# An attention and FFN block on one core: K in two rings of 512-key tiles, thinner FFN filling, one matmul for the rows of -max

## The chip, the core and the metric

One NeuronCore of a Trainium2 chip runs the whole kernel in one launch. TensorE (PE) multiplies matrices into eight PSUM banks, VectorE (DVE) and ScalarE (ACT) work on SBUF and PSUM, GpSimd (POOL) on SBUF alone; SyncE (SP) and POOL issue most DMAs. The engines run side by side, each in the order of its own instructions, and wait for each other by semaphores. The metric is the device time of one execution in microseconds, from the first to the last instruction.

## What is computed

A block with adaptive layer norm: attention with 32 heads of 16 channels over 2048 tokens of 512 channels, and a gated FFN with 1792 hidden channels, all in float32. The reference, cut:

```python
qkv = (x @ wqkv).reshape(B, S, 3, H, Dh)          # S = 2048, H = 32, Dh = 16
p = softmax(einsum("bhqd,bhkd->bhqk", q, k) * Dh ** -0.5)
A = einsum("bhqk,bhkd->bhqd", p, v)               # ... @ wo
B = (silu(h @ w_gate) * (h @ w_up)) @ w_down
mod = silu(c) @ w_mod                             # sa, ca, ga, sb, cb, gb
x = x + ga * A(layernorm(x) * (1 + ca) + sa)
x = x + gb * B(layernorm(x) * (1 + cb) + sb)
```

Operands of most matmuls are split in a high and a low part; three products (high-high, high-low, low-high) give each result.

## The kernel before, in words

**Stages.** First the projections to q, k, v: q and k go to DRAM in split parts, v stays in SBUF. Then attention in 32 units of 16 steps. A unit is 512 query rows (a chunk, four of them) and one group of four heads; units 0 to 7 are chunk 0, and so on. A step is one key tile of 128 keys for the four heads, in four pairs. After the last unit a tail finishes chunk 2 and does chunk 3's output projection and FFN.

**A pair** (pair_of) is two matmuls side by side on PE, on different 64 rows of the array: a score matmul (L506) of the current unit, with 48 split channels and 2 more rows that hold -max, and a max matmul (L479) some 20 steps ahead. ACT takes the exp of the score (L508), DVE the maximum over 512 keys of the other (L481). When a unit's maxima are complete, max_rows turns them to rows by matmuls with `ident` and `minus` (L491 to L493), and a DMA on SP puts them into the two rows of `qop`, four to five steps before that unit's first score.

**PV** (pv_step, L521) multiplies probabilities by v, in column tiles of 32; half a step at a time ("half"), two steps behind the scores.

**Plain and filled.** Where no FFN work is ready, plain runs windows of three pairs and one or two halves of PV; scores have three PSUM banks (4, 5, 6), max matmuls four. filled runs a group: pairs, with so many terms of an FFN job behind each as a tuple says, then up to six halves of PV. One term is two matmuls side by side on 64 rows each (L718), called a filler pair here. In a group banks 3 and 6 hold the job's sums, scores have banks 4 and 5 only, max matmuls 0 to 2. `TWO = (0, 3, 2, 2, 2, 2, 1, 0)` is a group of eight pairs (two steps) with 12 filler pairs, `ONE = (0, 3, 3, 0)` one of four pairs with 6. A gate_up job (24 filler pairs) takes two TWO, a down job (12) two ONE. A job accumulates in two half phases: in the first, sum 0 takes rows 0 to 63 and sum 1 rows 64 to 127, in the second the other way round. In TWO and ONE the half phase changes where a group ends, with PV between.

**Order around it.** The emitted order is the program's own (manual schedule). STARTS gives the step at which a finished chunk's output projection (out_pair) begins: four TWO groups, then NORM plain steps and three for layer norm, then the FFN jobs, then plain steps to the next chunk. The last 20 steps have no max matmuls; there ALONE exchanges the tuples.

**Unit end** (close_unit). The sums of exps come out of PV; SP fetches them into `dn` (L532), K and q of three units ahead start, DVE takes the reciprocal three steps later (L536), it goes to DRAM and back as `rb`, POOL multiplies (L548) and stores. Seven steps after a chunk's last unit its output is loaded again, two later split.

**Memory.** K of one head group lies in one of three tiles `kop` of 2048 keys; activations (`oT`, `hT`) in one pair `act`.

Of the kernel before, what the change touches and what calls it, by code (L numbers as in the profile page):

```python
# [19 lines left out]
P = 128  # L20
# [26 lines left out]
REST = 24  # L47
NORM = 9
STARTS = (147, 275, 403)
TWO = (0, 3, 2, 2, 2, 2, 1, 0)  # L50
ONE = (0, 3, 3, 0)
ALONE = {TWO: ((0, 4, 0, 4, 0, 4, 0, 0), (4, 5, 0, 1, 5, 0, 4, 1)), ONE: ((0, 6, 0, 0), (4, 5, 4, 0))}

# [48 lines left out]
def block_kernel(ctx, tc, x, wqkv, wo, w_gate, w_up, w_down, c, w_mod, out):  # L102
# [22 lines left out]
    minus = const.tile([P, P], F32, name="minus")  # L125
    eps_t = const.tile([P, 1], F32, name="eps_t")
    quad = const.tile([P, 1], F32, name="quad")
    modc = const.tile([P, 4, NK], F32, name="modc")
# [86 lines left out]
    kop = [vp.tile([P, 2, S], F32R, name="kop0"), None, None]  # L215
# [47 lines left out]
    nc.gpsimd.tensor_scalar_mul(minus, ident, -1.0)  # L263
# [137 lines left out]
    def load_parts(dst, src, g, c0, c1, second=nc.sync):  # L401
        heads = src[g * 64:(g + 1) * 64, :, c0:c1].rearrange("(s b d) r c -> b (d r) s c", s=2, b=2)
        for b in range(2):
            (second if b else nc.sync).dma_start(dst[64 * b:64 * b + KR].bitcast(F32), heads[b])

    def load_k0(ci):
        load_parts(kop[0][:, :, ci * CW:(ci + 1) * CW], kd, 0, ci * CW, (ci + 1) * CW)
# [3 lines left out]
    for b in range(2):  # L411
        nc.sync.dma_start(kop[0][64 * b + KR:64 * b + KR + 2].bitcast(F32).rearrange("p s (a c) -> p (s a) c", c=CW),
                          ones[:, None, :].to_broadcast([2, 2 * NC, CW]))
    kq = [(w, m) for m in range(NK) for w in (1, 0)]
    for ci in range(NC - 1):
# [12 lines left out]
        for i, _ in enumerate(sm.jobs(jobs)):  # L428
# [6 lines left out]
            if i == 40:  # L435
                load_k0(ci)
# [13 lines left out]
    kop[1] = pb.tile([P, 2, S], F32R, name="kop1", bufs=1)  # L450
    pf = None
    qop, mx, pts, pv, o_, due, res = {}, {}, {}, {}, {}, {}, {}
    posts = []
    n = 16 * NU
    last = NC - 1

    def ones_rows(k):
        for b in range(2):
            rows = slice(64 * b + KR, 64 * b + KR + 2)
            nc.sync.dma_start(kop[k][rows].bitcast(F32), kop[0][rows].bitcast(F32))  # L460

    def load_k(u):
        load_parts(kop[u % 3], kd, u % NG, 0, S, nc.gpsimd if u > 2 else nc.sync)

    def load_q(u):
        ci, g = divmod(u, NG)
        qop[u] = pb.tile([P, 2, CW], F32R, name="qop", tag="qop", bufs=3)
        load_parts(qop[u], qd, g, ci * CW, (ci + 1) * CW, nc.gpsimd if u > 2 else nc.sync)

    def max_one(r):  # L470

        u, t = divmod(r // 4, 16)
        b, e = 1 - r % 4 // 2, r % 2
        s, qt, kc = t // 8, t // 2 % 4, t % 2 * 2 + e
# [4 lines left out]
        nc.tensor.matmul(pm, qop[u][rows, s, qt * P:(qt + 1) * P], kop[u % 3][rows, s, kc * CW:(kc + 1) * CW],  # L479
# [3 lines left out]
    def max_rows(u):  # L483
# [3 lines left out]
        nm = pb.tile([P, 16], F32R, name="nm", tag="nm")  # L487

        def rows():
            pr = bank("pr")[0:16, 0:2 * P]  # L490
            nc.tensor.matmul(pr[:, 0:P], nm.bitcast(F32), ident, start=True, stop=True)  # L491
            nc.tensor.matmul(pr[:, P:2 * P], m, minus, start=True, stop=False)
            nc.tensor.matmul(pr[:, P:2 * P], nm.bitcast(F32), minus, start=False, stop=True)  # L493
            mr = pb.tile([16, 2, P], F32R, name="mr", tag="mr", bufs=1)
            nc.scalar.copy(mr, pr.rearrange("p (r q) -> p r q", r=2))
            for r in range(2):
                nc.sync.dma_start(qop[u][KR + r:KR + r + 65:64].bitcast(F32), mr[:, r, :].bitcast(F32))
        side.extend([lambda: None, lambda: None, lambda: nc.scalar.mul(nm, m, -1.0), lambda: None, rows])

    def score(i, h):  # L500
# [5 lines left out]
        nc.tensor.matmul(sp, kop[u % 3][rows, h // 2, kt * P:(kt + 1) * P], qop[u][rows, h // 2, :],  # L506
# [120 lines left out]
    class Chunk:  # L627
# [15 lines left out]
        def load_wo(self, places=None):  # L643
            self.wo = places or [as_wo(tile_gu()) for _ in range(NK // 2)]
            for k, w in enumerate(self.wo):
                (nc.sync if self.ci == 0 else nc.gpsimd).dma_start(w.bitcast(F32), wo_dr[k])

        def load_gu(self, f):
            if f < NF and f not in self.loaded:
                self.loaded.add(f)  # L650
                self.w[f] = self.places[f % len(self.places)] if self.places else tile_gu()
                nc.sync.dma_start(self.w[f].bitcast(F32), gu_dr[f])
# [56 lines left out]
    def accumulate(outs, lhs, rhs, nk, after, halves, by_k=False):  # L709
# [3 lines left out]
        if halves:  # L713
            for ph in range(2):
                for j, (k, a, b) in enumerate(terms):
                    for e in range(2):
                        rows = slice(64 * (ph ^ e), 64 * (ph ^ e) + 64)
                        nc.tensor.matmul(outs[e], lhs(e, a, k)[rows], rhs(b, k)[rows],  # L718
                                         start=(ph == 0 and j == 0), stop=(ph == 1 and j == z))
# [32 lines left out]
    def out_pair(ch, t0, outs, halves):  # L752
        return accumulate(outs, lambda e, a, k: ch.oT[a][:, k, (t0 + e) * P:(t0 + e + 1) * P],
                          lambda b, k: ch.wo[k // 2][:, b, k % 2, :], NK,
                          lambda: posts.append(lambda: add_o(ch, t0, outs, True)), halves)

    def out_terms(ch, t, pt, ks):
        for k in ks:
            for a, b in ((0, 0), (0, 1), (1, 0)):
                nc.tensor.matmul(pt, ch.oT[a][:, k, t * P:(t + 1) * P], ch.wo[k // 2][:, b, k % 2, :],  # L760
                                 start=(k == 0 and a == b == 0), stop=(k == NK - 1 and a == 1))

    def gate_up(ch, f, outs, halves):
# [5 lines left out]
        def after():  # L769
# [3 lines left out]
            def later():  # L773
# [10 lines left out]
        return accumulate(outs, lambda e, a, k: w[:, 2 * e + a, k, :], lambda b, k: ch.hT[b][:, k, :], NK, after,  # L784
                          halves)

    def down(ch, m, t0, outs, halves):
# [7 lines left out]
        def after():  # L795
# [4 lines left out]
            if t0:  # L800
# [4 lines left out]
                          lambda b, k: wd[:, b, k, :], FG, after, halves, m == NF // FG - 1)  # L805
# [4 lines left out]
    def begin(ci):  # L810
        x2 = pf.tile([P, 4, D], F32, name="x2", tag="x2", bufs=1)
# [247 lines left out]
```

## Time and profile before

| what | value |
|---|---|
| three runs, median (lowest to highest) | 1922.31 us (1921.94 to 1923.35) |
| the profiled execution, span | 1926.2 us |
| PE, DVE, ACT, POOL busy | 1876.4, 1541.1, 1250.8, 418.6 us |
| mean granted TensorE clock | 0.984 |
| step 0 to 147 (chunk 0's attention) | 188.3 to 566.3 us |
| last unit's end, tail | about 1762 us, to 1926.2 |

The span is that of one execution; it is 0.2% over the median. Rows of a timeline give start, duration, engine, line, operation, tiles, shapes, count and, in brackets, the idle time before and what ended it. A window's row gives its length, then for each engine the busy time with the number of instructions, then the granted clock, the DMA share and GB/s. "bank" is any PSUM bank. PEld is PE's weight load.

### The profile page before, as it was taken

How to read it: one execution, taken by the hardware profiler on the slowest of the kernel's cores; microseconds unless marked ns; L12 is line 12 of the kernel's file. 1: busy time of each engine (PE TensorE's matmuls, PEld its weight loads, DVE VectorE, ACT ScalarE, POOL GpSimd, SP SyncE). 2: the span in 40 equal slices, each digit the busy share in tenths (PEclk: the TensorE clock that was granted, in tenths of full speed). 3: DMA queues.
4: the chain of work that ended last, by engine and by line, in shares of the span. 5: the costliest groups of instructions: out<-in, count | busy, mean ns of one | idle time of the engine just before them, and what ended most of it. 6: DMA issues, size and time to landing. Idle time of an engine off the chain costs nothing.

```text
span 1926.2 us, 40835 instructions
## 1 busy us (share of the span) xinstructions
PE 1876.4 (97%) x16996; PEld 1149.1 (60%) x16996; DVE 1541.1 (80%) x2558; ACT 1250.8 (65%) x2330; POOL 418.6 (22%) x504
## 2 busy tenths in 40 slices
PE   7999999999999999999899999999899999999999
PEld 5766444444455666666455666666455466667787
DVE  5458998999989888888789888888799988841643
ACT  4222887788877766667677766776677876674211
POOL 3000344555322211111123111111133011021200
PEclk9999999999999999999899999999899999999999
DMA  8764766667753534553544544453543354253642
GB/s 299 265 219 121 187 161 161 190 180 185 192 90 74 141 99 113 148 133 84 130 81 90 121 114 131 116 141 76 135 81 76 54 141 119 73 177 122 237 194 109
DMA packets 78340, 267.60 MB, mean 139 GB/s; under 512 B 17364, under 2 KB 22484, under 8 KB 57476
## 3 DMA queue, kind: packets, MB, share of 16 engines
q1 hardware_dynamic: 58188, 173.81, 31.7%
q0 software_dynamic: 19280, 90.39, 19.5%
q8 instruction: 133, 2.18, 0.5%
q10 hardware_dynamic: 688, 0.80, 0.1%
q14 instruction: 51, 0.42, 0.1%
HBM read 201.85 MB, written 62.13 MB: 137 GB/s over the span
## 4 chain that ended last, share of the span: by engine, by line
PE 89%; DMA 5%; DVE 3%; ACT 2%; SPq 0%; issue 0%; ACTq 0%; DVEq 0%
PE bank L521 25%; PE bank L506 20%; PE bank L718 18%; PE bank L479 9%; PE bank L727 7%; PE bank L209 6%; DMA dn<-o 4%; DVE mx L481 1%; PE bank L760 1%; PE bank L491 1%; DVE stt L743 1%; PE bank L162 0%; PE bank L703 0%; DMA wm_ab<-in_w_mod 0%; PE bank L493 0%
## 5 line engine op out<-in xcount | busy, mean ns | idle before, releaser
L481 DVE TENSOR_REDUCE mx<-bank 128x1 f32<-128x512 f32 x2048 | 1285.6, 683 | 146.9 <-PE bank L479 97.7
L479 PE MATMUL bank<-kop,qop 48*128 48x512 f32 x2048 | 766.2, 439 | 26.4 <-DVE mx L481 25.0
L506 PE MATMUL bank<-qop,kop 50*128 50x512 f32 x2048 | 757.4, 433 | 3.8 <-DMA qop<-mr 0.9
L506 PEld LDWEIGHTS bank<-qop,kop 50*128 50x128 f32 x2048 | 349.0, 187 | 315.6 <-issue 54.5
L479 PEld LDWEIGHTS bank<-kop,qop 48*128 48x128 f32 x2048 | 347.3, 187 | 59.2 <-DVE mx L481 42.4
L718 PE MATMUL bank<-act,wgu 64*128 64x512 f32 x1872 | 295.4, 393 | 0.0
L718 PEld LDWEIGHTS bank<-act,wgu 64*128 64x128 f32 x1872 | 184.3, 187 | 32.6 <-issue 0.2
L548 POOL TENSOR_TENSOR on<-o,rb 128x512 f32<-128x512 f32 x31 | 39.8, 1283 | 527.4 <-DMA rb<-d_dr 379.4
L718 PE MATMUL bank<-wd,mid 64*128 64x512 f32 x912 | 130.5, 392 | 0.0
L779 POOL CAST mid<-m 128x512 fp32r<-128x512 f32 x40 | 24.5, 612 | 345.4 <-PE bank L479 164.8
L209 PE MATMUL bank<-hT,wqs 128*128 128x512 f32 x384 | 95.8, 400 | 2.3 <-ACT hT L328 1.0
L718 PEld LDWEIGHTS bank<-wd,mid 64*128 64x128 f32 x912 | 88.7, 186 | 15.3 <-issue 0.7
L209 PEld LDWEIGHTS bank<-hT,wqs 128*128 128x128 f32 x384 | 70.4, 188 | 24.3 <-issue 6.1
L775 DVE SCALAR_TENSOR_TENSOR q<-th,bank 128x512 f32<-128x512 f32 x56 | 38.1, 681 | 56.8 <-ACT th L771 56.8
L771 ACT ACTIVATE th<-bank 128x512 f32<-128x512 f32 x56 | 33.3, 594 | 58.5 <-PE bank L727 58.4
L791 DVE TENSOR_TENSOR x<-bank,x 128x512 f32<-128x512 f32 x84 | 53.9, 685 | 19.6 <-PE bank L718 19.6
L369 DVE TENSOR_TENSOR prt<-bank,prt 128x512 fp32r<-128x512 f32 x32 | 22.0, 689 | 45.5 <-ACT prt L367 45.5
L367 ACT CAST prt<-bank 128x512 fp32r<-128x512 f32 x32 | 18.8, 586 | 58.6 <-PE bank L209 46.8
L777 DVE TENSOR_TENSOR m<-bank,q 128x512 f32<-128x512 f32 x56 | 38.7, 692 | 21.1 <-PE bank L727 19.1
L727 PE MATMUL bank<-wd,mid 128*128 128x512 f32 x216 | 52.3, 395 | 0.5 <-DVE mid L780 0.3
L780 POOL TENSOR_TENSOR mid<-m,mid 128x512 fp32r<-128x512 f32 x40 | 51.5, 1288 | 3.3
L718 PE MATMUL bank<-wgu,act 64*128 64x512 f32 x288 | 47.9, 395 | 0.1
(6282 smaller groups left out, 5196.9 us busy)
## 6 DMA issues: line engine op xcount, KB each, us to landing
wgu<-gu_dr SPq DMA_DIRECT2D x48, 1024.0 KB
wd<-wd_dr SPq DMA_DIRECT2D x28, 1024.0 KB
kop<-kd SPq DMA_DIRECT2D x33, 768.0 KB
kop<-kd POOLq DMA_DIRECT2D x29, 768.0 KB, 8.4
gu_dr<-wgu POOLq DMA_DIRECT2D x14, 1024.0 KB, 4.9
kd<-prt SPq DMA_DIRECT2D x16, 512.0 KB
qd<-prt SPq DMA_DIRECT2D x16, 512.0 KB
kop<-gu_dr SPq DMA_DIRECT2D x8, 1024.0 KB
```

The costliest lines, as they stand in the source:

```text
L209: nc.tensor.matmul(pt, lhs(a, k), rhs(b, k), start=(n == 0), stop=(n == 3 * nk - 1))
L479: nc.tensor.matmul(pm, qop[u][rows, s, qt * P:(qt + 1) * P], kop[u % 3][rows, s, kc * CW:(kc + 1) * CW], start=True, stop=True)
L481: nc.vector.tensor_reduce(mx[u][:, b, s, qt, kc:kc + 1], pm, op=ALU.max, axis=AX.X)
L506: nc.tensor.matmul(sp, kop[u % 3][rows, h // 2, kt * P:(kt + 1) * P], qop[u][rows, h // 2, :], start=True, stop=True)
L521: nc.tensor.matmul(pv[u][32 * h:32 * h + 32, cols], v_flat[:, e0:e0 + 32], p_[h][:, cols], start=(kt == 0 and half == 0), stop=(kt == 15), ...
L548: mul.tensor_mul(on, o, rb)
L718: nc.tensor.matmul(outs[e], lhs(e, a, k)[rows], rhs(b, k)[rows], start=(ph == 0 and j == 0), stop=(ph == 1 and j == z))
L727: nc.tensor.matmul(outs[e], lhs(e, a, k), rhs(b, k), start=(j == 0), stop=(j == z))
L775: nc.vector.scalar_tensor_tensor(q, th, 1.0, outs[0], op0=ALU.add, op1=ALU.mult)
L777: nc.vector.tensor_mul(m32, outs[1], q)
L780: (nc.gpsimd if slow else nc.vector).tensor_sub(mid[:, 1, :], m32, mid[:, 0, :].bitcast(F32))
L791: nc.vector.tensor_add(ch.x2[:, t, :], outs[e], ch.x2[:, t, :])
```

## The change

Six edits, together:

- **K in two rings.** Three tiles of 2048 keys become two rings of four tiles of 512; each is loaded for the unit two ahead as soon as the unit before has used it (four loads a unit, all on SP, as are q's). Max matmuls now take the key tiles in order.
- **A second pair of activation buffers**, by the parity of the chunk. x and wo of the next chunk are loaded at the end of the chunk's jobs, attention output in pairs of units.
- **Filling over more groups.** Most gate_up jobs take three groups THIN (24 filler pairs in 6 steps), the others two TWO as before; THICK says from which job on. A down job takes one group of eight pairs, DOWN or LATE. The plain steps between chunks and before the last down go; STARTS and REST follow.
- **Half phases inside a group.** Where the half phase changes within a group, ACT copies one column of both sums (`seen`) first, so that the second phase's matmuls come after the first's.
- **One matmul for the rows of -max**, of 32 columns; the low part comes from one DVE operation, and the matmul stands at the end of a window or group (flush).
- **Unit end later**: reciprocal after five steps, not three, and what follows it.

```diff
-STARTS = (147, 275, 403)
+STARTS = (144, 272, 400)
+REST = 12
+THICK = (12, 12, 8)
 TWO = (0, 3, 2, 2, 2, 2, 1, 0)
-ONE = (0, 3, 3, 0)
+DOWN = (0, 3, 3, 0, 0, 3, 3, 0)
+LATE = (0, 0, 3, 3, 0, 0, 3, 3)
+THIN = ((0, 1, 1, 2, 1, 1, 1, 1), (0, 2, 2, 0, 0, 2, 2, 0), (0, 2, 1, 2, 1, 1, 1, 0))
...
-    kop = [vp.tile([P, 2, S], F32R, name="kop0"), None, None]
+    kop = [[vp.tile([P, 2, CW], F32R, name=f"kop0{c}") for c in range(NC)], None]
...
-            pr = bank("pr")[0:16, 0:2 * P]
-            nc.tensor.matmul(pr[:, 0:P], nm.bitcast(F32), ident, start=True, stop=True)
-            nc.tensor.matmul(pr[:, P:2 * P], m, minus, start=True, stop=False)
-            nc.tensor.matmul(pr[:, P:2 * P], nm.bitcast(F32), minus, start=False, stop=True)
+            pr = bank("pr")[0:32, 0:P]
+            nc.tensor.matmul(pr, nm.rearrange("p r h -> p (r h)").bitcast(F32), ident, start=True, stop=True)
...
             for ph in range(2):
+                for e in range(2 if trade and ph else 0):
+                    nc.scalar.copy(seen[:, e:e + 1], outs[e][:, 0:1])
                 for j, (k, a, b) in enumerate(terms):
...
-        at(i + 3, lambda: res.__setitem__(u, out_b(u, nc.sync, *res[u])))
-        at(i + 4, lambda: res.__setitem__(u, out_r(u, nc.sync, *res[u])))
-        at(i + 5, lambda: out_c(u, nc.gpsimd, nc.gpsimd, *res.pop(u)))
...
+        at(i + 5, lambda: res.__setitem__(u, out_b(u, nc.sync, *res[u])))
+        at(i + 6, lambda: res.__setitem__(u, out_r(u, nc.sync, *res[u])))
+        at(i + 8, lambda: out_c(u, nc.gpsimd, nc.gpsimd, *res.pop(u)))
+        if u % 2 and u < NU - 2:
+            at(i + 10, lambda: chunks[u // NG].load_o(nc.gpsimd, (u % NG // 2,)))
+            at(i + 12, lambda: chunks[u // NG].split_o((u % NG // 2,)))
+
+    for u in range(NU - 2):
+        for c in range(NC):
+            at(16 * u + 4 * c + 3, lambda u=u, c=c: load_k(u + 2, c))
...
+    def window(ch, job, args):
+        if job is down:
+            return (LATE if args == (NF // FG - 1, 0) else DOWN,)
+        return (TWO,) * 2 if args[0] >= THICK[ch.ci] else THIN
...
-                plain(WIN)
-            work = job(ch, *args, outs, True)
-            for _ in range(2):
-                filled(TWO if job is gate_up else ONE, work)
+                chunks[ci + 1].load_wo()
+            places = window(ch, job, args)
+            work = job(ch, *args, outs, True, *[True] * (len(places) > 2))
+            for group in places:
+                filled(group, work)
```

What this moves on PE, at a down job of chunk 2. Before, the first half phase ends here and its group with it (bank_66 and bank_69 are the sums, 67 and 68 the scores, 63 to 65 the maxima, 70 PV):

```order
L718 MATMUL bank_69<-wd,mid 128x512
L506 MATMUL bank_68<-qop,kop_1425 128x512 [waits Activation_49]
L479 MATMUL bank_63<-kop_87,qop 128x512 [waits DVE_49]
L521 MATMUL bank_70<-pt__15178,v_flat 32x256
L521 MATMUL bank_70<-pt__15194,v_flat 32x256
L521 MATMUL bank_70<-pt__15183,v_flat 32x256
L521 MATMUL bank_70<-pt__15207,v_flat 32x256
```

And now, at the same place of a job:

```order
L729 MATMUL bank_69<-wd,mid 128x512
L504 MATMUL bank_68<-qop,kop_88 128x512 [waits Activation_49]
L474 MATMUL bank_63<-kop_971,qop 128x512 [waits DVE_49]
L504 MATMUL bank_67<-qop,kop_88 128x512 [waits Activation_49]
L474 MATMUL bank_64<-kop_971,qop 128x512 [waits DVE_49]
L504 MATMUL bank_68<-qop,kop_88 128x512 [waits Activation_49]
L474 MATMUL bank_65<-kop_971,qop 128x512 [waits DVE_49]
L729 MATMUL bank_66<-wd,mid 128x512 [waits Activation_49]
L729 MATMUL bank_69<-wd,mid 128x512 [waits Activation_49]
```

The PV between the half phases is gone; three pairs without filling stand there, and the second phase's first matmuls wait for ACT. What they wait for stands on ACT, here in a THIN group of chunk 0, the exps of pairs r3 to r6 (rows of the changed kernel; before there is nothing between two exps at this place):

```order
L506 ACTIVATE pt__6833<-bank_68 128x512 [waits PE_49]
L506 ACTIVATE pt__6840<-bank_67 128x512 [waits PE_49]
L506 ACTIVATE pt__6845<-bank_68 128x512 [waits PE_49]
L725 COPY seen<-bank_66 128x1
L725 COPY seen<-bank_69 128x1
L506 ACTIVATE pt__6856<-bank_67 128x512 [waits PE_49,Activation_49]
```

The copies come behind the exp of pair r5, whose score PE issues just before the matmuls that wait. On SP, a unit's end before (the sums `dn`, K and q, the reciprocal's way out and back):

```order
L532 DMA dn<-o 128x1x16 [waits Activation_49]
L404 DMA kop_87<-kd 48x2x2048 [waits DMAHW4_49,PE_49]
L404 DMA qop<-qd 48x2x512 [waits DMASW5_49,PE_49]
L537 DMA d_dr<-dn 128x16 [waits DMAHW6_49,DVE_49]
L542 DMA rb<-d_dr 128x1x512 [waits DMAHW7_49,DMAHW6_49,Pool_49]
```

And now:

```order
L530 DMA dn<-o 128x1x16 [waits DMAHW1_49,Activation_49]
L407 DMA qop<-qd 48x2x512 [waits DMAHW2_49]
L407 DMA qop<-qd 48x2x512 [waits DMAHW3_49]
L407 DMA kop_969<-kd 48x2x512 [waits DMAHW4_49,PE_49]
L407 DMA kop_969<-kd 48x2x512 [waits DMAHW5_49,PE_49]
L535 DMA d_dr<-dn 128x16 [waits DMAHW6_49,DVE_49]
L407 DMA kop_970<-kd 48x2x512 [waits DMAHW7_49,PE_49]
L407 DMA kop_970<-kd 48x2x512 [waits DMAHW0_49,PE_49]
L540 DMA rb<-d_dr 128x1x512 [waits DMAHW6_49,DMAHW1_49,Pool_49]
```

The large K load behind `dn` is gone; smaller ones stand between the steps of the unit's end, and q's second half has come over from POOL.

More of the change, by code (lines that the diff above doesn't have):

```diff
@@ L449, in block_kernel @@
     pb = ctx.enter_context(tc.tile_pool(name="pb", bufs=2, reuse_waits="tile"))
-    kop[1] = pb.tile([P, 2, S], F32R, name="kop1", bufs=1)
+    kop[1] = [pb.tile([P, 2, CW], F32R, name=f"kop1{c}", bufs=1) for c in range(NC)]
     pf = None
     qop, mx, pts, pv, o_, due, res = {}, {}, {}, {}, {}, {}, {}
-    posts = []
+    posts, tails = [], []
     n = 16 * NU
     last = NC - 1
[L457 to L463, printed above, removed]
     def load_q(u):
@@ L478, in max_one @@
         pm = four("pm")
-        nc.tensor.matmul(pm, qop[u][rows, s, qt * P:(qt + 1) * P], kop[u % 3][rows, s, kc * CW:(kc + 1) * CW],
+        nc.tensor.matmul(pm, qop[u][rows, s, qt * P:(qt + 1) * P], kop[u % 2][kc][rows, s, :],
                          start=True, stop=True)
@@ L505, in score @@
         sp = bank("st_")
-        nc.tensor.matmul(sp, kop[u % 3][rows, h // 2, kt * P:(kt + 1) * P], qop[u][rows, h // 2, :],
+        nc.tensor.matmul(sp, kop[u % 2][kt // 4][rows, h // 2, kt % 4 * P:(kt % 4 + 1) * P], qop[u][rows, h // 2, :],
                          start=True, stop=True)
@@ L826, in hook, with flush @@
             posts.pop(0)()
+    def flush():
+        while tails:
+            tails.pop(0)()
     late = sm.jobs([proj_T(last, w, m) for w, m in kq[:1] + kq[2:]] + [proj_T(last - 1, w, m) for w, m in kq[6:]] +
                    [proj_T(last, *kq[1])] + [proj_v(4 * ci + t) for ci in (last - 1, last) for t in range(4)])
-    ones_rows(1)
+    for c, t in enumerate(kop[1]):
+        for b in range(2):
+            own = slice(64 * b + KR, 64 * b + KR + 2)
+            nc.sync.dma_start(t[own].bitcast(F32), kop[0][c][own].bitcast(F32))
     load_q(0)
     take(late, 22)
-    load_k0(last)
+    load_k(0, last)
     take(late, 26)
@@ L880, in block_kernel @@
         if i == -LEAD + 3:
-            load_k(1)
+            for c in range(NC):
+                load_k(1, c)
             load_q(1)
@@ L925, in end_steps, with plain @@
             ended += 1
-    def plain(steps, tails=()):
+    def plain(steps, ends=()):
         nonlocal four, bank
@@ L934, in plain @@
                 pair_of()
-            if w >= 4 * steps // WIN - len(tails):
-                tails[w - 4 * steps // WIN](four())
+            if w >= 4 * steps // WIN - len(ends):
+                ends[w - 4 * steps // WIN](four())
+            flush()
             pvs((HALVES[(w - 2) % 4] if done > 8 else 0) + (w == 4 * steps // WIN - 1), True)
@@ L1005, in block_kernel @@
     rest = whole(chp, chp.jobs)
+    ch.x2 = v_flat[:, 0:4 * D].rearrange("p (t d) -> p t d", t=4)
     ch.load_x2(nc.gpsimd)
+    ch.places = [[kop[r][2 * k + e] for e in range(2)] for r in (1, 0) for k in range(2)]
+    ch.ahead = 4
+    for f in range(2):
+        ch.load_gu(f)
     for t in range(4):
@@ L1023, in block_kernel @@
     take(rest, 48)
-    ch.places = [tile_gu() for _ in range(2)]
-    for u in (NU - 3, NU - 2):
-        ch.places += [kop[u % 3][:, k, :].rearrange("p (a k c) -> p a k c", a=4, k=NK) for k in range(2)]
-    ch.ahead = 4
-    for f in range(ch.ahead):
+    ch.places += [tile_gu() for _ in range(2)]
+    for f in range(2, ch.ahead):
         ch.load_gu(f)
```

119 lines of the change are left out of this document (61 added, 58 removed).

## The prediction

> **What bounds the kernel now.** I read the page first, its span, busy shares and the chain's shares by engine:
>
> ```profile
> span 1926.2 us, 40835 instructions
> PE 1876.4 (97%) x16996; PEld 1149.1 (60%) x16996; DVE 1541.1 (80%) x2558; ACT 1250.8 (65%) x2330; POOL 418.6 (22%) x504
> PE 89%; DMA 5%; DVE 3%; ACT 2%; SPq 0%; issue 0%; ACTq 0%; DVEq 0%
> ```
>
> PE carries 89% of the chain, but that is an average over stages. A step is one key tile of one unit, 4 exps on ACT, so windows of the exp's line (L508) count steps: the x in brackets divided by four. Rows: the first stretch (147 steps), a pure stretch of it (16 steps), the FFN stretch of chunk 0 (87 steps), and the stretches behind chunks 0 and 1 (21 steps each).
>
> ```profile
> 188.30:566.30 378.00, 305.78 (x588) 0.96 0.67 170
> 394.80:433.60 38.80, 33.26 (x65) 1.00 0.67 161
> 628.40:931.30 302.90, 200.59 (x349) 1.00 0.45 114
> 931.30:995.70 64.40, 43.97 (x85) 0.87 0.59 131
> 1360.30:1425.80 65.50, 43.98 (x85) 0.87 0.57 130
> ```
>
> A plain step costs 38.8 / 16 = 2.43 us; a step with FFN filling 302.9 / 87 = 3.48. The same two kinds of stretch with all engines (PE, PEld, DVE, ACT, POOL):
>
> ```profile
> 394.80:433.60 38.80, 38.73 (x396) 18.14 (x384) 38.71 (x67) 33.90 (x68) 19.32 (x20) 1.00 0.67 161
> 628.40:931.30 302.90, 302.69 (x3133) 197.83 (x3130) 261.36 (x415) 210.70 (x380) 47.11 (x56) 1.00 0.45 114
> ```
>
> In a plain step DVE is full (38.71 of 38.80); in a filled one PE is (302.69 of 302.90) and DVE has 14% to spare. A balance between the two is what the thinner filling could win. Whether it does is decided inside one group, so I read one TWO group (8 pairs, 12 filler pairs, then 4 halves of PV) row by row, PE's scores, weight loads that waited, and exps:
>
> ```profile
> 775.21 0.49 PE L506 MATMUL bank<-qop,kop 50*128 50x512 f32 x1
> 775.55 0.38 PE L506 MATMUL bank<-qop,kop 50*128 50x512 f32 x1
> 775.83 0.61 ACT L508 ACTIVATE pt__8607<-bank 128x512 f32<-128x512 f32 x1
> 776.32 0.60 ACT L508 ACTIVATE pt__8612<-bank 128x512 f32<-128x512 f32 x1
> 776.49 0.18 PEld L506 LDWEIGHTS bank<-qop,kop 50*128 50x128 f32 x1 [0.28 <-ACT pt__8607 L508]
> 777.02 0.60 ACT L508 ACTIVATE pt__8623<-bank 128x512 f32<-128x512 f32 x1
> 777.29 0.39 PE L506 MATMUL bank<-qop,kop 50*128 50x512 f32 x1
> 777.71 0.60 ACT L508 ACTIVATE pt__8632<-bank 128x512 f32<-128x512 f32 x1
> 778.01 0.39 PE L506 MATMUL bank<-qop,kop 50*128 50x512 f32 x1
> 779.12 0.60 ACT L508 ACTIVATE pt__8650<-bank 128x512 f32<-128x512 f32 x1
> 779.77 0.18 PEld L506 LDWEIGHTS bank<-qop,kop 50*128 50x128 f32 x1 [0.19 <-ACT pt__8650 L508]
> 779.85 0.42 PE L506 MATMUL bank<-qop,kop 50*128 50x512 f32 x1
> 782.07 0.18 PEld L506 LDWEIGHTS bank<-qop,kop 50*128 50x128 f32 x1 [0.41 <-issue]
> ```
>
> These rows give the six numbers of my sums. A pair or a filler pair takes PE 0.235 (777.29 to 778.01 is a pair and two fillers). The second pair of a group comes 0.34 after the first. An exp starts 0.62 after its score in a group's first pair, 0.53 where PE had waited (776.49, 777.02), 0.42 else. Two exps are 0.49 apart at least. In a filled group scores have two banks only, so a score waits for the exp two pairs back: **0.65 after that exp's start** (779.12, 779.77). From the last pair to the next group's first: 2.22. Walked with these, TWO comes to 6.75 us; its rows say 6.86 (775.21 to 782.07). ONE, half of it, in the same view:
>
> ```profile
> 711.75 0.18 PEld L506 LDWEIGHTS bank<-qop,kop 50*128 50x128 f32 x1 [0.41 <-issue]
> 715.30 0.18 PEld L506 LDWEIGHTS bank<-qop,kop 50*128 50x128 f32 x1 [0.41 <-ACT pt__7841 L508]
> ```
>
> 3.55, so 7.10 for the two that a down took.
>
> **Downs.** One DOWN group has the work of two ONE, but its second half phase stands behind two one-element copies on ACT, and ACT takes them only after the exp of pair r5 (the rows of PE and ACT in the section on the change). Walk: r0 0, r1 0.34, three fillers, r2 1.28, three fillers, r3 2.22. No fillers now, so the bank loop rules: exp of r2 starts 1.81, r4 at 2.46; exp of r3 2.64, r5 at 3.29; its exp 3.82. The copies' price is not in the trace; the nearest row is ACT's smallest other operation, and another small one, reading PSUM, is the upper bound:
>
> ```profile
> L498 ACT ACTIVATE nm<-m 128x16 fp32r<-128x16 f32 x32 | 6.9, 217 | 0.9 <-DVE m L486 0.9
> L495 ACT CAST mr<-bank 16x256 fp32r<-16x256 f32 x32 | 11.6, 362 | 3.4 <-PE bank L493 3.4
> ```
>
> With 0.217 each, overlapping like exps (0.11), they end at 4.63 and PE goes on at 4.68 instead of 3.52: **1.16 us of wait**. Behind it on PE stand the fillers, r6, r7 and the PV, all that PE has. Then r6 at 5.38, r7 at 6.32, next group at 8.54. So a down costs 1.44 more: 34 x 1.44 = +49, and the four in the last 20 steps, where there are no max matmuls, I put alike, +6. Bounds of the wait: 0.95 if the copies cost nothing (the exp still has to end), 1.45 with 0.362 each.
>
> The Trainium skill's page "TensorEngine Tiling (Array Packing)", section Key Properties, says that a change of tiling mode drains TensorE, which speaks for the longer group, since it has one such change less. The trace agrees: TWO and two ONE hold the same work, 6.86 against 7.10. By that rule alone downs would get 0.24 shorter, -8 in all; by the walk they get longer, since what is saved at the PV is smaller than the wait.
>
> **Gates.** 32 of the gate_up jobs (12, 12 and 8) go from two TWO groups in 4 steps to three THIN groups in 6. Walked the same way, THIN's first group has its pairs at 0, 0.34, 1.28, 1.76, 2.46, 2.95, 3.54, 4.12, one filler, 2.22: 6.57. Eight fillers instead of twelve save almost nothing, since pairs cannot follow one another faster than the bank loop lets them. The third group is 6.34. The second has the copies: r5 at 3.05, its exp 3.58, PE goes on at 4.44, r7 at 5.6: 7.80. Sum 20.7. Before, the same 6 steps were two TWO (13.72) and two plain steps (4.86): 18.58. So +2.1 each, 32 x 2.1 = +68.
>
> **Unit end.** The reciprocal of the softmax sums waits on DVE for its DMA, and everything queued behind it, the max reductions and then PE, waits too. The wait list, the worst case of it (DVE, then PE), and the DMA's issue:
>
> ```profile
> DVE dn L536 <- DMA dn<-o: 34.3, 8, 9.5
> 940.44 0.58 SPq L532 DMA_DIRECT2D dn<-o  x1
> 959.08 0.25 DVE L536 RECIPROCAL dn<-dn 128x16 f32<-128x16 f32 x1 [9.51 <-DMA dn<-o]
> 959.93 0.79 PE L479 MATMUL bank<-kop,qop 48*128 48x512 f32 x1 [8.63 <-DVE mx L481]
> ```
>
> Two more steps (4.9 us at 2.43) cover the short waits, and at the chunk's end the x and wo loads no longer start with this DMA. What it cost is read from the stretches: 64.4 and 65.5 against 21 x 2.43 = 51.0 are 28 us, the first stretch 378.0 against 147 x 2.43 = 357.2 is 21 (the DVE waits named explain about 9 of that, and PE, at reduced clock after each, more). I take -26 and -18: **-44**; bounds 0 and -49. Next late is then the bank loop, not another DMA.
>
> **Rows of -max.** Three matmuls become one, of 32 columns:
>
> ```profile
> 926.68 0.39 PE L491 MATMUL bank<-ident,nm 128*16 128x128 f32 x2
> 927.44 0.50 PE L506 MATMUL bank<-qop,kop 50*128 50x512 f32 x1
> L486 DVE TENSOR_REDUCE m<-mx 128x16 f32<-128x64 f32 x32 | 6.9, 216 | 0.9
> ```
>
> 0.76 between rows and next pair becomes a third, 0.25: -0.5 in the 23 units whose rows fall where PE is full, **-12**; nothing where DVE is. The added DVE operation is priced as the small reduction, 0.216: at most +2 over the 9 units in plain steps, hidden elsewhere by DVE's 14%.
>
> **At nothing:** the K pieces. They move from two queues (SP and POOL) to SP alone, 8 issues a unit:
>
> ```profile
> kop<-kd POOLq DMA_DIRECT2D x29, 768.0 KB, 8.4
> ```
>
> A piece has about seven steps (17 us) until its first max and holds a quarter of that load; uncovered it would stop PE at up to 128 places. SP's waits are for scores already issued, and behind them on SP wait the rows' and sums' DMAs, with a step or more of room. The second pair of activation buffers only removes waits at chunk ends, counted above. The tail after the last unit, which is PE alone, keeps its work:
>
> ```profile
> 1802.33 113.84 PE bank L727 x496
> ```
>
> **Sum**, against the profiled execution: +49 + 6 + 68 - 44 - 12 = +67, so 1926.2 + 67 = 1993. The three runs' median, 1922.31, is 0.998 of that span; scaled, **1989 us**. Steps are conserved: the 24 plain steps that each chunk gives up are the ones in THIN's sixes.
>
> **Rivals.**
> - *The copies' wait is covered* (PE would have stood anyway, for DVE or for ACT). Place: the filler behind the copies, 70 times; price 1.16 each, 81 in all: 1993 - 81 = 1912, scaled 1908, faster. Against it: DVE has 14% to spare in these stretches and ACT 30%. It decides where the real wait is under 0.2 us, for 70 x (1.16 - 0.2) is what the change loses. 10%.
> - *The filling does balance*: PE's work alone counts. THIN is then 3 x (6.86 - 4 x 0.235) = 17.8 against 18.58, 32 x -0.8 = -26; a down, as much work as one TWO, is 6.86 against 7.10, 34 x -0.24 = -8. With -12 and -44 that is -90, scaled 1833. Against it stands the row at 779.77: with one filler between, a pair already waits for the exp. 5%. The drain rule above would put the downs here.
> - *The rows of -max come late too*: they now leave at a group's end, one group (8.8 us with its PV) before the first score that needs them. Where their DMA takes over 7 us, PE stands at each unit's start; 2 us in 23 units would give 2035. 8%.
> - *The change doesn't do what it says at the unit end*: the sums are still late, since their DMA shares SP with more issues. +44: 2033. 5%.
>
> **How the numbers follow.** Forecast 72%, its own range 1955 to 2020 by the wait's bounds (70 x -0.21 and +0.29) and half of the unit end. The range leaves out the balance case, most of the covered case and the worst of the two late ones, and reaches down for a wait partly covered: 1930 to 2028. A measurement of this kernel tells about 0.2% (4 us) from no change. Faster by more: the first two rivals less a little, 14%; the same 3%; slower 83%.
>
> **What would show it.** Right: a DOWN group of 8.3 to 8.7 from first score to next first score, PE's idle before the wd fillers ended by ACT's one-element copies, THIN groups of 6.3 to 6.6 and 7.8, DVE's share falling in the FFN stretches, no reciprocal waiting on its DMA. Wrong: THIN groups near 6, a copy that ends before PE gets there, or a filled step under 3.3 us.

## The result, and the profile after

| | before | changed |
|---|---|---|
| median (lowest to highest) | 1922.83 us (1921.94 to 1923.71) | **2074.16 us** (2065.61 to 2085.42) |
| ratio to before, 95% interval | 1 | **1.0792** (1.0755 to 1.0829) |
| profiled execution, span | 1926.2 us | 2083.5 us |
| step 0 to 144 | 370.5 us | 381.9 us |
| 108 steps with chunk 0's FFN, with chunk 1's | 367.3, 368.2 us | 413.0, 404.0 us |
| from the copy of the last unit's output (`o`) to the end | 161.5 us | 171.8 us |

The changed kernel is slower by 151 us; 67 were forecast, and the range ended at 2028. The profiled execution of the changed kernel is the longest of its four, so its stretches are up to 0.5% longer than the median. The page's top lines, of the changed kernel:

```profile
span 2083.5 us, 41412 instructions
PE 1929.9 (93%) x16868; PEld 1159.9 (56%) x16868; DVE 1539.5 (74%) x2590; ACT 1252.4 (60%) x2470; POOL 386.2 (19%) x447
PE 70%; DVE 19%; ACT 7%; DMA 2%; issue 1%; SPq 0%; ACTq 0%; DVEq 0%
```

PE fell from 89% of the chain to 70%, DVE rose from 3% to 19%, ACT from 2% to 7%: PE now waits for others. Windows of the exp's line (now L506), first the 144 steps of chunk 0's attention, then the two FFN stretches, with ACT's time in exps and the granted clock behind it:

```profile
189.80:571.70 381.90, 298.32 (x577) 0.95 0.52 164
635.50:1048.50 413.00, 242.87 (x432) 0.98 0.32 100
1112.20:1516.10 403.90, 242.82 (x432) 1.00 0.32 102
```

A step of the first stretch, where 2.43 us was the pace of a plain one, takes 381.9 / 144 = 2.65. The forecast had that stretch getting shorter. The wait list of the changed kernel says for whom PE waits (engine, line, what for: us in total, times, longest; PEld and PE are the weight load and the matmul of the same places, so the two are not added):

```profile
PEld bank L729 <- ACT seen L725: 74.5, 70, 1.3
PE bank L729 <- ACT seen L725: 52.5, 70, 1.0
PEld bank L519 <- ACT o L523: 26.4, 28, 1.2
PE bank L486 <- DVE nm L493: 24.1, 14, 3.2
PE bank L519 <- ACT o L523: 14.2, 20, 0.8
DVE dn L534 <- DMA dn<-o: 11.8, 1, 11.8
PE bank L504 <- DMA qop<-mr: 2.9, 1, 2.9
```

In the kernel before, the same list has for the copy of `o`

```profile
PEld bank L521 <- ACT o L525: 5.3, 17, 0.6
```

and none for the other two. So three waits are new or grown: 70 times for the copies `seen`, 14 times for the DVE operation of the rows of -max, and 20 to 28 times for the copy of a unit's output `o`. Each has a place in the timeline. First the copies, in the second group of a THIN three (start, duration, engine, line, what, and in brackets the idle time before):

```profile
685.70 0.50 PE L504 MATMUL bank<-qop,kop 50*128 50x512 f32 x1
...
688.82 0.50 PE L504 MATMUL bank<-qop,kop 50*128 50x512 f32 x1 [0.19 <-ACT pt__7325 L506]
...
690.06 1.26 PE L729 MATMUL bank<-act,wgu 64*128 64x512 f32 x4 [0.74 <-ACT seen L725]
...
695.11 0.50 PE L504 MATMUL bank<-qop,kop 50*128 50x512 f32 x1
```

ACT, in the same group:

```profile
689.36 0.60 ACT L506 ACTIVATE pt__7335<-bank 128x512 f32<-128x512 f32 x1
689.85 0.22 ACT L725 COPY seen<-bank 128x1 f32<-128x1 f32 x2
```

The score of pair r5 starts on PE at 688.82, its exp at 689.36, the copies 0.49 behind that, and the filler that waits for them at 690.06: the very walk of the prediction, with 0.22 for both copies instead of 0.33. From first score to next first score the group takes 9.41, though 7.80 were walked; the group at the same place in chunk 1's jobs takes 7.88. What the other 1.6 are is shown at the end. The second place, the rows of -max, in a plain step of the first stretch:

```profile
388.25 3.07 DVE L476 TENSOR_REDUCE mx<-bank 128x1 f32<-128x512 f32 x5
...
389.28 0.23 ACT L496 ACTIVATE nm<-m 128x16 fp32r<-128x16 f32 x1
...
391.24 0.99 DVE L493 SCALAR_TENSOR_TENSOR nm<-m,nm 128x16 fp32r<-128x16 f32 x1
392.15 0.68 DVE L476 TENSOR_REDUCE mx<-bank 128x1 f32<-128x512 f32 x1
392.37 0.27 PE L486 MATMUL bank<-ident,nm 128*32 128x128 f32 x1 [2.21 <-DVE nm L493]
```

ACT's half of `nm` is ready at 389.51, but DVE takes its own operation only at 391.24, after the max reductions queued before it, and PE, whose matmul for the rows is next in its order, waits for 2.21 us. No max matmul runs on PE meanwhile, so DVE gets nothing new either: over the whole stretch it waits 27.1 us for PE (1.5 us in the run below that has three matmuls). The engine that was full in this stretch runs dry. And then the clock, from windows of PE over the same place (length, busy time and count, granted clock, DMA share, GB/s):

```profile
391.00:392.00 1.00, 0.00 (x0) 1.00 0.00 0
392.00:393.00 1.00, 0.63 (x10) 1.00 0.00 0
393.00:394.00 1.00, 1.00 (x8) 0.61 0.49 197
...
398.00:400.00 2.00, 2.00 (x16) 0.50 0.35 121
400.00:402.00 2.00, 2.00 (x26) 0.99 0.30 90
```

After the stall PE runs at half its clock for 6.8 us, and catches nothing up. The third place, half a step of PV at a unit's end:

```profile
683.61 0.38 PE L519 MATMUL bank<-pt__7191,v_flat 128*32 128x256 f32 x1
684.70 0.40 PE L519 MATMUL bank<-pt__7221,v_flat 128*32 128x256 f32 x1 [0.71 <-ACT o L523]
```

The next unit's PV needs the bank that ACT is copying out. Last, the chain of waits behind the last unit, in the tail:

```profile
1911.75 0.59 ACT o L523
...
1912.37 9.46 DMA dn<-o
...
1921.85 0.26 DVE dn L534
```

The DMA of the sums, 8 KB, takes 9.46 us there. Before, at the same place, its issue and the reciprocal were 3.02 apart:

```profile
1765.36 1.12 ACTq L532 DMA_DIRECT2D dn<-o  x1
...
1768.38 0.25 DVE L536 RECIPROCAL dn<-dn 128x16 f32<-128x16 f32 x1 [7.22 <-DMA dn<-o]
```

Four places, then, besides the groups' own length: the experiments take them one at a time.

### The profile page after: what moved, and what is told of

Read it like the earlier page. It is cut to its first block, busy times and chain, and to the rows that moved or that the text cites. A ratio compares the mean times of both kernels' runs of the same rounds, so it can differ in the third digit from the quotient of the medians.

```text
span 2083.5 us, 41412 instructions
## 1 busy us (share of the span) xinstructions
PE 1929.9 (93%) x16868; PEld 1159.9 (56%) x16868; DVE 1539.5 (74%) x2590; ACT 1252.4 (60%) x2470; POOL 386.2 (19%) x447
## 4 chain that ended last, share of the span: by engine, by line
PE 70%; DVE 19%; ACT 7%; DMA 2%; issue 1%; SPq 0%; ACTq 0%; DVEq 0%
DVE mx L476 18%; PE bank L729 18%; PE bank L519 17%; PE bank L504 16%; PE bank L739 6%; PE bank L213 6%; PE bank L474 5%; ACT o L523 1%; DMA dn<-o 0%; PE bank L486 0%; ACT seen L725 0%; PE bank L166 0%; PE bank L712 0%; DVE stt L755 0%; DMA wm_ab<-in_w_mod 0%
## 5 line engine op out<-in xcount | busy, mean ns | idle before, releaser
L504 PE MATMUL bank<-qop,kop 50*128 50x512 f32 x2048 | 788.8, 442 | 34.6 <-DMA qop<-mr 2.9
L474 PE MATMUL bank<-kop,qop 48*128 48x512 f32 x2048 | 792.3, 445 | 3.6 <-DVE mx L476 1.9
L504 PEld LDWEIGHTS bank<-qop,kop 50*128 50x128 f32 x2048 | 354.3, 188 | 410.5 <-issue 76.9
L474 PEld LDWEIGHTS bank<-kop,qop 48*128 48x128 f32 x2048 | 352.1, 188 | 24.4 <-DVE mx L476 13.4
L729 PE MATMUL bank<-act,wgu 64*128 64x512 f32 x1872 | 340.5, 404 | 23.4 <-ACT seen L725 23.4
L729 PEld LDWEIGHTS bank<-act,wgu 64*128 64x128 f32 x1872 | 197.0, 190 | 48.8 <-ACT seen L725 33.5
L729 PE MATMUL bank<-wd,mid 64*128 64x512 f32 x912 | 140.7, 404 | 29.1 <-ACT seen L725 29.1
L729 PEld LDWEIGHTS bank<-wd,mid 64*128 64x128 f32 x912 | 96.9, 187 | 47.3 <-ACT seen L725 41.0
L213 PEld LDWEIGHTS bank<-hT,wqs 128*128 128x128 f32 x384 | 71.0, 190 | 24.8 <-issue 6.2
L739 PE MATMUL bank<-act,kop 128*128 128x512 f32 x240 | 57.0, 394 | 0.0
```

Source lines behind the costliest of these rows:

```text
L213: nc.tensor.matmul(pt, lhs(a, k), rhs(b, k), start=(n == 0), stop=(n == 3 * nk - 1))
L504: nc.tensor.matmul(sp, kop[u % 2][kt // 4][rows, h // 2, kt % 4 * P:(kt % 4 + 1) * P], qop[u][rows, h // 2, :], start=True, stop=True)
L739: nc.tensor.matmul(outs[e], lhs(e, a, k), rhs(b, k), start=(j == 0), stop=(j == z))
```

## Experiments

Each ratio is to the kernel before on the same chip; its median was 1922.5 to 1923.4 us on the three chips used, so times from different chips are compared below. Single parts were undone in the changed kernel, done alone in the one before, or put back into the best version found on the way.

**The copies earlier.** The copies stand where the first half phase ends, not where the second begins; they still order the two.

```diff
-                for e in range(2 if trade and ph else 0):
-                    nc.scalar.copy(seen[:, e:e + 1], outs[e][:, 0:1])
...
+                    if trade and ph == 0 and j == z:
+                        for e in range(2):
+                            nc.scalar.copy(seen[:, e:e + 1], outs[e][:, 0:1])
                     yield
```

> The changed kernel, with the two one-element copies emitted at the end of the first half phase instead of at the start of the second, so that ACT takes them before the exps of the three pairs without filling. Theory (PE stands behind the copies): the 70 waits of about 1.1 us go, 77 us, and some of the clock dips that follow them: 1985 to 2005, and no wait of the filling on the copies in the trace. Rival (the pairs would have waited for the exps anyway, in the loop of two score banks): under 30 us gained, above 2044.

Measured: **1993.15 us** (1987.69 to 1995.91), ratio 1.0354 (1.0331 to 1.0377), so 81.0 less than the changed kernel. PE's fillers no longer wait, as the largest group of them shows (busy, mean ns, then idle time before, 23.4 in the changed kernel):

```profile
L727 PE MATMUL bank<-act,wgu 64*128 64x512 f32 x1872 | 325.4, 392 | 0.0
```

It follows that the place of the copies in ACT's order, not the copies themselves, cost 81, as much as the 70 x 1.16 of the prediction. The agreement is in part luck: where the clock is full, a DOWN group is 8.53 long with the copies late and 7.48 with them early (medians of 32), so a place costs 1.05, as the wait list says (74.5 / 70 = 1.06) and as the walk gives with 0.22 for both copies; 70 of these are 74. For the other 7 there is half clock: 9 of the 32 middle groups of a THIN three ran into it with the copies late, none with them early. But 1993 is still 70 over before.

**The filling of before** in the changed kernel (two TWO a gate, two ONE a down, the plain steps back).

```diff
-REST = 12
-THICK = (12, 12, 8)
+REST = 27
+THICK = (0, 0, 0)
-DOWN = (0, 3, 3, 0, 0, 3, 3, 0)
+ONE = (0, 3, 3, 0)
...
-            return (LATE if args == (NF // FG - 1, 0) else DOWN,)
+            return (ONE,) * 2
```

> The changed kernel with the filling of before alone: gates in two TWO, downs in two ONE, no copies, the plain steps back; rings, buffers, rows and unit end stay changed. By the prediction's terms this takes back 68 + 49 + 6 = 123 us: 1951; with fewer clock dips 1935 to 1955. Rival (most of the loss sits in the rows of -max, the unit's end or the tail): above 1990.

Measured: **1934.76 us** (1929.21 to 1938.19), ratio 1.0054 (1.0032 to 1.0075), the lower end of what was expected. The filling's price in all is 139 us; what is left of the change is still no gain, though the unit end alone was to bring 44.

**The rows of -max by three matmuls** in the changed kernel, taken from the side queue at once, without the DVE operation.

```diff
-            pr = bank("pr")[0:32, 0:P]
-            nc.tensor.matmul(pr, nm.rearrange("p r h -> p (r h)").bitcast(F32), ident, start=True, stop=True)
+            pr = bank("pr")[0:16, 0:2 * P]
+            nc.tensor.matmul(pr[:, 0:P], nm.bitcast(F32), ident, start=True, stop=True)
+            nc.tensor.matmul(pr[:, P:2 * P], m, minus, start=True, stop=False)
+            nc.tensor.matmul(pr[:, P:2 * P], nm.bitcast(F32), minus, start=False, stop=True)
...
-        side.extend([lambda: None, lambda: None, lambda: nc.scalar.mul(nm[:, 0, :], m, -1.0), lambda: None, rest])
+        side.extend([lambda: None, lambda: None, lambda: nc.scalar.mul(nm, m, -1.0), lambda: None, rows])
```

> The changed kernel with the rows of -max as before: three matmuls, no DVE operation, taken from the side queue at once and not at the group's end. Theory (the new DVE operation and the late place make PE wait at every unit): 25 to 60 us less than the changed kernel, 2015 to 2050, and the slow steps 13 to 15 of each unit in the first stretch go. The prediction's term says the other way: 12 us more, about 2086.

Measured: **2049.37 us** (2046.66 to 2051.70), ratio 1.0652 (1.0636 to 1.0667): 24.8 less than the changed kernel, where the prediction's term had 12 more. A window over the same 144 steps of its profile (PE, PEld, DVE, ACT, POOL; then clock, DMA share, GB/s):

```profile
189.10:540.00 350.90, 350.42 (x3496) 164.45 (x3496) 348.70 (x594) 305.57 (x603) 161.85 (x158) 1.00 0.57 178
```

350.9 instead of 381.9, at full clock, with PE and DVE both full. The edit that was to save 12 costs 25, and it costs it in the first stretch, where the prediction had at most 2. Of the 31 us there, PE's waits for the rows (17.4 for DVE, 2.9 for the DMA) explain at most 20, and 37 us at half clock, which the run with three matmuls doesn't have, at most 19; so by these bounds each has a share of 11 or more.

**The rows three pairs later**, to see whether the matmul only stood too early:

```diff
-            tails.append(rows)
-        side.extend([lambda: None, lambda: None, lambda: nc.scalar.mul(nm[:, 0, :], m, -1.0), lambda: None, rest])
+        side.extend([lambda: None, lambda: None, lambda: nc.scalar.mul(nm[:, 0, :], m, -1.0), lambda: None, rest, lambda: None, lambda: None, lambda: tails.append(rows)])
```

> The changed kernel, its one matmul for the rows of -max kept, but taken three pairs later, so that the DVE operation before it is done when PE gets there. Theory (PE waits for the new DVE operation, which stands behind max reductions): the first stretch falls from 382 to 356 us or less, in all 20 to 31 us less than the changed kernel, 2043 to 2054. Rival (what costs is that the rows reach qop too late): still later rows make it slower, above 2080.

Measured: **2073.56 us** (2070.05 to 2079.95), ratio 1.0792 (1.0764 to 1.0821): no gain, and the expectation missed. Its wait list:

```profile
PE bank L504 <- DMA qop<-mr: 8.5, 3, 3.9
PE bank L486 <- DVE nm L493: 3.3, 4, 1.2
```

PE's wait for DVE fell from 24.1 to 3.3, but now the rows reach `qop` too late three times (8.5 us, against 2.9 in one): there is little room between the maxima and the first score that needs them. These two lines alone would leave a gain of some 15 us, and the first stretch of this profile is 371.5 long, 10 less than the changed kernel's, where 26 or more were expected. Why the medians are equal all the same is not shown.

**The unit end alone**, in the kernel before (reciprocal at i + 5, and what follows it later by as much).

```diff
-        at(i + 3, lambda: res.__setitem__(u, out_b(u, nc.sync, *res[u])))
-        at(i + 4, lambda: res.__setitem__(u, out_r(u, nc.sync, *res[u])))
-        at(i + 5, lambda: out_c(u, nc.gpsimd, nc.gpsimd, *res.pop(u)))
+        at(i + 5, lambda: res.__setitem__(u, out_b(u, nc.sync, *res[u])))
+        at(i + 6, lambda: res.__setitem__(u, out_r(u, nc.sync, *res[u])))
+        at(i + 8, lambda: out_c(u, nc.gpsimd, nc.gpsimd, *res.pop(u)))
```

> The kernel before, with the unit's end later alone (reciprocal after five steps, the rest in step with it). Theory (the reciprocal's wait for its DMA is worth what the stretches say): the first stretch loses 18 us, the two chunk ends some 7 each, since x and wo still load there: 1888 to 1895. Rival (another transfer is late next, or PE had the time anyway): within 5 us of 1922.

Measured: **1902.19 us** (1898.65 to 1909.08), ratio 0.9891 (0.9868 to 0.9915): a gain of 21, where 27 to 34 were expected. Its wait for the sums, which was 34.3 us in 8 before:

```profile
DVE dn L536 <- DMA dn<-o: 19.4, 4, 6.9
```

Steps 0 to 147 took 359.1 instead of 378.0; the two 108-step stretches 362.9 and 362.1, a gain of 4 and 6 where some 7 each were expected here, and 13 each in the prediction with the loads moved too. At the chunks' ends the later steps alone are not enough.

**Rings, second buffers and unit end**, with the filling, the starting steps and the rows of before:

```diff
-STARTS = (144, 272, 400)
-REST = 12
-THICK = (12, 12, 8)
+STARTS = (147, 275, 403)
+REST = 24
+THICK = (0, 0, 0)
```

> Rings, second buffers, loads and unit end of the change, with the filling, the starting steps and the rows of before. By the stretches: the first one 351 instead of 371 us for 144 steps, the two chunk ends 13 us less each, tail 10 us more as in the changed kernel: 1922 - 19 - 26 + 10 = 1887. Rival (rings and SP's extra issues have a price of their own): above 1902, what the later unit end alone gave.

Measured: **1891.23 us** (1889.71 to 1892.31), ratio 0.9842 (0.9825 to 0.9859). The 108-step stretches are 354.4 and 354.9, another 8 less each: with the x and wo loads moved and the smaller K loads the whole gain comes (which of the two brings it was not separated). From the copy of the last unit's output to the end it took 169.2, against 161.5 before.

**The same, with the tail's first loads late.** The changed tail starts two loads of gate and up weights (1 MB each) ahead of the output projection; here they stand behind it as before.

```diff
-    for f in range(2):
-        ch.load_gu(f)
     for t in range(4):
         out_terms
...
-    for f in range(2, ch.ahead):
+    for f in range(ch.ahead):
```

> The same, and the tail's first two loads of FFN weights go back behind the output projection. Theory (these loads delay the small DMAs of the last unit's end): 6 to 13 us less than the run before it, 1874 to 1881. Rival (the tail is longer for another reason): within 3 us of it.

Measured: **1884.84 us** (1884.66 to 1886.40), ratio **0.9809** (0.9794 to 0.9823). The loads cost 6.4 us: from the issue of the sums' DMA to the reciprocal it was 7.68 us with them ahead, and is 1.94 now. This version beats both kernels; its page:

```profile
span 1884.3 us, 41357 instructions
PE 1858.3 (99%) x16996; PEld 1150.5 (61%) x16996; DVE 1537.5 (82%) x2558; ACT 1250.1 (66%) x2330; POOL 387.6 (21%) x448
PE 95%; DVE 2%; ACT 2%; DMA 1%; issue 0%; SPq 0%; ACTq 0%
```

The next three start from it and put back one edit each.

**The thinner filling, with early copies.** THIN, DOWN and LATE of the change, nothing else that was found to cost (the kernel that ran is the changed one with the earlier copies, three matmuls, the starting steps of before, REST 9 and the late tail loads).

```diff
-STARTS = (144, 272, 400)
-REST = 12
+STARTS = (147, 275, 403)
+REST = 9
```

> The changed kernel's thin filling without its side costs: copies early, rows as before, tail loads late, chunks starting at odd steps so that a unit's end falls on a group's end. Theory (the loop of two score banks sets the pace of a thin group): gates 32 x 1.1 and downs 38 x 0.2 more than the run before it, about 40 us, 1915 to 1925. Rival (the thin filling balances PE and DVE once the waits are gone): under 1877.

Measured: **1949.17 us** (1947.40 to 1951.04), ratio 1.0142 (1.0126 to 1.0158): 64.3 over the best version, where 30 to 40 were expected. The first weight load of each group of one THIN three and of the group behind it, and one in between that waits for an exp:

```profile
703.89 0.18 PEld L503 LDWEIGHTS bank<-qop,kop 50*128 50x128 f32 x1 [0.41 <-issue]
...
707.45 0.18 PEld L503 LDWEIGHTS bank<-qop,kop 50*128 50x128 f32 x1 [0.35 <-ACT pt__8018 L505]
...
710.51 0.18 PEld L503 LDWEIGHTS bank<-qop,kop 50*128 50x128 f32 x1 [0.41 <-issue]
...
717.29 0.18 PEld L503 LDWEIGHTS bank<-qop,kop 50*128 50x128 f32 x1 [0.41 <-issue]
...
723.69 0.18 PEld L503 LDWEIGHTS bank<-qop,kop 50*128 50x128 f32 x1 [0.41 <-issue]
```

6.62, 6.78, 6.40: a group with eight fillers is hardly shorter than TWO with twelve (6.86 before), with no filler that waits for a copy in it. The bank loop keeps the pace. That is 19.80 against the 18.58 of two TWO and two plain steps: 32 x 1.22 = 39. A DOWN group took 7.47 instead of 7.10, 34 x 0.37 = 13. The other 12 are spread: the profile has up to 4 in the downs of the last 20 steps (7.06 each in the mean, against 6.11 in the best version), 4 to 5 in waits for the copy of `o` (9.6 us instead of 5.1), since REST 9 sets chunk 2's jobs on even steps, and 4 behind the last copy of `o` (166.8 against 162.7), which is not explained. So some 8 of the 64 belong to the starting step and the tail rather than to thin groups.

**Even starting steps** in the best version:

```diff
-STARTS = (147, 275, 403)
-REST = 24
+STARTS = (144, 272, 400)
+REST = 27
```

> The fastest version so far (rings, buffers, unit end; filling, rows and tail of before), with the chunks starting at even steps as in the changed kernel (144, 272, 400). Then a unit's last PV and the next unit's first stand in the same run of PV, and PE waits there for ACT to take the old sums out of bank 7. Theory: about 1.05 us in each of the 23 units that end in filled groups, 1905 to 1912 against 1885. Rival (PE would wait at the group's start anyway): within 5 us of 1885.

Measured: **1895.72 us** (1894.44 to 1897.87), ratio 0.9859 (0.9845 to 0.9873): 10.9 more, about half of what was expected. PE's waits for the copy of `o`, which were 5.1 us in 17 on the weight loads in the best version:

```profile
PEld bank L517 <- ACT o L521: 14.2, 20, 1.2
PE bank L517 <- ACT o L521: 6.5, 9, 0.8
```

The start sets how windows and groups fall on the units: from an even step the four halves behind a group hold a unit's last PV and the next unit's first, with ACT's copy of 0.59 between them and nothing else for PE to do.

**One matmul for the rows** in the best version, from the side queue two pairs behind the DVE operation, so neither at a group's end nor three pairs late:

```diff
-        side.extend([lambda: None, lambda: None, lambda: nc.scalar.mul(nm, m, -1.0), lambda: None, rows])
+        side.extend([lambda: None, lambda: None, lambda: nc.scalar.mul(nm[:, 0, :], m, -1.0), rest, lambda: None, rows])
```

> The fastest version so far with the change's one matmul for the rows of -max, but taken from the side queue two pairs after the DVE operation, not at a group's end. The prediction's term alone (0.5 us of PE in 23 units): 1873. Theory (in plain steps PE runs ahead of DVE, so it still waits for the DVE operation behind the max reductions): up to 1 us in each of the 9 first units given back, 1873 to 1884. Rival (any DVE operation in that path costs more than two matmuls): above 1890.

Measured: **1913.47 us** (1907.07 to 1917.56), ratio 0.9954 (0.9937 to 0.9971): 28.6 more than the best version. The rival was right. Its groups for the DVE operation and for the matmul (the last figures: idle time before, and what ended it):

```profile
L492 DVE SCALAR_TENSOR_TENSOR nm<-m,nm 128x16 fp32r<-128x16 f32 x32 | 13.0, 406 | 2.0 <-ACT nm L494 2.0
L485 PE MATMUL bank<-ident,nm 128*32 128x128 f32 x64 | 13.1, 288 | 28.4 <-DVE nm L492 19.5 <-ACT pt__17977 L504 0.9 <-ACT pt__3353 L504 0.9
```

And the first of the three matmuls in the best version, which needs ACT's `nm` alone:

```profile
L487 PE MATMUL bank<-ident,nm 128*16 128x128 f32 x64 | 12.6, 278 | 1.2 <-ACT nm L494 0.9
```

PE stands 28.4 us before the one and 1.2 before the other. Most of the loss, 24.2, lies in steps 0 to 147 (382.1 against 357.9), at a granted clock of 0.95 against 1.00. The waits there are 14.9 us, and 34 us at half clock can cost at most 17; how the 24 divide between the two was not separated.

## Why the prediction was wrong, step by step

The step that failed is the rows of -max: -12 was put, and it costs 25. Beside it the walk of the groups was 22 short, and the starting steps and the tail's loads, 17 together, stood at nothing. The terms against what the runs give for each:

| step | forecast | measured | between which two |
|---|---|---|---|
| copies' wait, 70 times | +81 | +81.0 | changed, copies earlier |
| groups without that wait | +42 | +64.3 | thinner filling with early copies, best version |
| rows of -max | -12 | +24.8; +28.6 | changed, three matmuls; one matmul in the best version, best version |
| starting steps | 0 | +10.9 | even starts, best version |
| tail's first loads | 0 | +6.4 | rings and unit end, best version |
| unit end, rings, buffers | -44 | -38.0 | best version, before (1922.83) |
| **sum** | **+67** | **+149.4** (with 24.8) | changed, before: +151.3 |

The parts add up to within 2 us, and the four edits undone together, 2074.16 - 1949.17 = 125.0, give the 123.1 of the single ones. A single term is less certain than that: the filling undone at once gave 139.4, where its two rows here make 145.3, and the rows of -max cost 24.8 in one kernel and 28.6 in another.

- **What bounds the kernel, and the copies: right.** The place, the exp of the pair before and the count of 70 are as walked, and a DOWN group of 8.53 was to be 8.3 to 8.7. The 1.16 was 0.1 too much for the two copies, and half clock, which the sum did not have, made up for it; that the total is 81.0 is luck. The rival of a covered wait falls.
- **Gates and downs: right in sign, too small.** 42 forecast without the copies (20.7 less 1.16, against 18.58, 32 times; 8.54 less 1.16, against 7.10, 34 times; 1 for the last four), 64 measured. A THIN three was walked 0.26 short (19.80 against 20.7 - 1.16), a down 0.09, together 11; the other 11 lies where no term was: the last downs, chunk 2's even steps, the tail. The rival that filling balances falls: with eight fillers a group is 6.4 to 6.8 long, not 5.9.
- **Unit end: right.** In the best version's profile steps 0 to 147 are 20.1 shorter (forecast 18), the two stretches 12.9 and 11.8 (forecast 26 for both); by the medians the whole gain is 38 of the 44. With the waits went the 27 us at half clock that the first stretch had before. The later steps alone gave 20.6 by the medians; the rest needed the loads of the change as well. In the changed kernel the reciprocal waits once for its DMA, in the tail (11.8), not in 8 places: the rival of sums still late falls.
- **Rows of -max: this step failed, in sign.** The prediction put "nothing where DVE is" full, and priced the added DVE operation "at most +2 over the 9 units in plain steps", as its duration. What counts is its place. DVE is full there and starts the operation only after the reductions already queued; PE waits with its matmul (17.4 us in that stretch); and while PE waits, nobody feeds DVE, which idles 27.1 us instead of 1.5. The time is lost for good, with half clock behind it. Nor did the 12 come where PE is full: with one matmul in the best version the two 108-step stretches are 355.3 and 357.2 long, against 354.4 and 356.4 with three. The rival of late rows had looked at the DMA at the end of this path; the wait is at its beginning. (Its 8.8 us for a group is 6.57 + 2.22, but the walk's 6.57 has the 2.22 of PV in it already.)
- **Starting steps: not in the sum.** The prediction has no term for STARTS. Where a unit's end falls in a run of PV decides whether PE has something else to do for the 0.59 us of the copy.
- **Tail: "keeps its work", and it did**; the order of its loads changed, and the sums' small DMA, issue to reciprocal, went from 3.02 to 9.48 us behind two loads of 1 MB. Worth 6.4.
- **K rings: at nothing, right as far as shown.** No wait of PE for a K load stands in the lists of the changed kernel or of the best version; no run has the rings alone.
- **Range.** It was made from the copies' bounds and half of the unit end. The unknown costs that it did not hold were a loss in the rows and the groups' walk, about 37 and 22: with these alone the time is 2048, past its end.

## What to carry to other kernels

When an edit trades work on one engine for a small operation on a full, in-order one, price the operation by the queue it joins and by who stands still behind it, not by its duration; if the one that stands still feeds the full engine, nothing hides it. The same holds for synchronising copies: put them in the queue as soon as their input exists, since 81 us hung on two small instructions standing three pairs too late. And thin a filling only where the filling sets the pace: a group whose pace comes from two banks in turn stays as long when a third of its filling is taken out.

## What the runs showed of the hardware that had not been expected

The granted clock falls to 0.50 for stretches of 3.4 us, or whole multiples of it. Windows of 1 us over the whole attention and tail, twice what the clock lacks to 1 summed, give 61 us at half clock in 8 stretches for the kernel before, 85 us in 20 for the changed one, 37 of these in its first stretch, and 3.4 us in a single one for the best version. One such stretch began behind a stall of 2.2 us (the rows above), others behind idle time in short pieces: the windows around the copies of the THIN group shown above, before and in it,

```profile
686.00:689.90 3.90, 3.09 (x20) 1.00 0.43 103
690.00:691.00 1.00, 0.94 (x5) 0.59 0.53 139
691.00:692.00 1.00, 1.00 (x8) 0.50 0.15 57
...
693.00:694.00 1.00, 1.00 (x17) 0.71 0.06 18
694.00:695.00 1.00, 1.00 (x24) 1.00 0.57 168
```

have PE idle for 0.81 of 3.9 us in all, and within the next microsecond the clock is halved. The Trainium skill's page "TensorE: Matmul & The Clock Gate", Part 1, describes a gate with a window of about 3.4 us, which the lengths here agree with; its rule of no idle gaps over about 3.4 us is too mild for this kernel, where half clock came behind a wait of 2.21 and behind these 0.81 in pieces, and no wait of PE in the list above was longer than 3.2. So small waits that come close together can cost more than their sum: that group is the one that took 9.41, where its like in chunk 1, at full clock, took 7.88.

The stretches do not follow every such wait. Of the 32 middle groups of a THIN three, all with the wait for the copies, 9 ran into half clock (9.3 to 9.6 long): 6 of chunk 0's 12, none of chunk 1's 12 (7.8 to 8.1), 3 of chunk 2's 8. All changes of the clock in a trace lie on one grid of 3.413 us; the stretches that begin at 690.2, 751.6 and 813.0 here are 61.4 apart, 18 steps of it. So it may be the place of a wait on this grid that decides; that was not tested. The spread of the changed kernel's runs, 20 us against 2 for the best version, goes with the clock: from the longest run to the shortest the mean granted clock was 0.979, 0.983, 0.985 and 0.986, and 0.007 of 2075 us, as an estimate of what the clock cost, is 15 of the 20.
